# Score products of the second attention layer in 64-row tiles, on block-diagonal pairs of keys

## The chip, the cores and the metric

The kernel runs on one core of a Trainium2 chip. The metric is the device time of one execution in microseconds (us). The times of before are 384.46 us as the median of 3 runs (383.48 to 384.55).

## The reference, cut to what matters

Four layers run one after the other on `x` of 2048 tokens by 448 features: attention (layer 0), gated MLP (layer 1), attention (layer 2), gated MLP (layer 3). Both attention layers have the same weights, and so have both MLP layers. All inputs are bf16.

```python
x = x + A(layernorm(x));  x = x + B(layernorm(x))
x = x + A(layernorm(x));  x = x + B(layernorm(x))

def A(x):                       # H = 16 heads of 28, window W = 8, dilation 2
    q, k, v = split(x @ wqkv)
    idx = pos[:, None] - 2 * arange(8)          # 8 keys of each query
    logits = where(idx >= 0, q . k[idx] * 28 ** -0.5, -1e9)
    return (softmax(logits) . v[idx]) @ wo

def B(x):
    return ((x @ w_gate) * (x @ w_up)) @ w_down
```

A query looks at 8 keys at distances 0, 2, ... 14 behind it.

## The kernel before, in words

**Tokens.** Even tokens are stored first and odd tokens behind them, 1024 each (`HALF`), so that the dilated window becomes a window of 8 neighbours in each half. The 2048 stored tokens are cut into 17 query blocks (`qb_info`): block 0 of 128 queries, and 16 of 120 queries that look at 128 keys. Blocks 1 and 2, 3 and 4 and so on are handled in pairs: 9 groups in each attention layer, the first with one block. The block that crosses from the even to the odd half is called `STRADDLE`.

**Stages.** `SEQ` lists the jobs. `A00` is chunk 0 of layer 0, and so on. An attention chunk makes the transposed normalised input `xnT` (`ln_chunk`), the keys and queries (`qk_chunk`, matmuls of L362 on `WQK`), the values (`v_group`, L362 on `WV`), and then for each group the scores (`attn_front`, matmuls of L842), exp on ScalarE (L849), a product with a mask on VectorE (L859), the product with the values (`attn_back`, L879), the sum and the division (L890 to L917), and the output projection (`y_blocks`, L362 on `wo_g`). The MLP chunks (`b_chunk`) make gate and up products (L362 on `WGU`; 14 units to a chunk of 512 tokens), ScalarE copies the gate (L970), VectorE multiplies (L973), and the down product follows (L362 on `WD`, with L934 that adds to `x_sb`).

**Tiles of TensorE.** Feature dimension 448 is 7 times 64 rows. So nearly every product runs in 64-row tiles: two matmuls of 64 rows by 128 columns lie side by side, one in the upper and one in the lower half of the array, each writing a bank of its own (`twin`, `twin_blocks`). The transposes at the head (L638) have the same form, with 64 streamed columns. Scores are another form: 28 rows (one head) by 64 keys, in 32-row tiles, 64 matmuls to a pair of blocks, into four banks. The product with the values has 64 rows by 32 columns, 64 matmuls to a pair.

**Keys, queries, values.** `qk` holds both for all 2048 tokens, a head in 28 of each 32 partitions; the four rows between carry a part of the values, which goes to DRAM (`vt`, DMAs of L741) and comes back transposed. Head 4*hc + b stands in partitions 32*b, chunk hc. Values are copied out of PSUM by one instruction for a pair of blocks (L824).

**Order.** The code adds operations one after the other (`sc.add`); the number of an operation is its place in that list. The order on each engine is written out by hand in `ORD`, a list of numbers per engine, and `BANK` gives the PSUM banks. `44!v` is operation 44, and the letter tells which of its waits stands last. `253+349@24.30.42` is a burst (the 64 short matmuls of 253) in which operation 349, broken into strips of 32 columns (L365) or 32 rows (L369), is mixed at the places named. Every engine works its list strictly in order. `plan_waits` leaves out waits that others cover. The costs given with `sc.add` served to make the lists; at run time they do nothing.

**Head.** TensorE runs 18 matmuls on zeros (L535, operations 44 to 61): 15 before the first transposes of `xn` (110 and 114, blocks 0 and 1) and 3 behind them, then the first keys and queries (199 on). Those need the transposed input, copied out by ScalarE and VectorE (L646), and the weights in `WQK`, spread out of `stage` by 8 copies (L544, operations 62 to 69: row chunk c, half w; the first two units need the four of w = 0). Six of the copies are GpSimd's: its list has 63, 62, 64, 68, 69 and later 65 among 16 small operations that build the masks (L515, L519).

Of the kernel before, what the change touches and what calls it, by code (L numbers as in the profile page):

```python
# [7 lines left out]
S = 2048  # L8
# [47 lines left out]
FILL = 9  # L56
ORD = {
# [56 lines left out]

# [9 lines left out]
class Sched:  # L124
# [21 lines left out]
    def schedule(self):  # L146
# [29 lines left out]
        for e in self.ENGS:  # L176
            for x in ORD[e].split():
                ids, _, hint = x.partition("!")
                ids, _, cuts = ids.partition("@")
                ids, _, pre = ids.partition("~")  # L180
                burst, *hosts = [self.ops[int(i)] for i in ids.split("+")]
                pre = int(pre or 0)
                if pre:
                    for op in hosts:
                        take(op, e)
                    order[e].append((hosts, [(op, n) for op in hosts for n in range(2 * pre)], hint[:1]))
                    hint = hint[1:]
                    take(burst, e)
                else:
                    for op in (burst, *hosts):  # L190
                        take(op, e)
                seq = [(burst, n) for n in range(len(burst.ins))]
                if hosts:
                    strips = self.strips(x, hosts, pre, len(cuts.split(".")))
                    done = pre + len(strips) // len(hosts)
                    seq, a = [], 0
                    for i, z in enumerate([int(c) for c in cuts.split(".")] + [len(burst.ins)]):
                        seq += [(burst, n) for n in range(a, z)]
# [4 lines left out]
                order[e].append(([burst] if pre else [burst, *hosts], seq, hint))  # L203
# [194 lines left out]
def build(nc, A_x, A_wqkv, A_wo, B_w_gate, B_w_up, B_w_down, out):  # L398
# [35 lines left out]
    ones32 = sb([128, 128], bf, "ones32")  # L434
    MK = sb([128, 3, 72], bf, "MK")
    ident = sb([128, 128], bf, "ident")
# [263 lines left out]
    def qk_chunk(li, j, prio):  # L700
# [5 lines left out]
        if li >= 2:  # L706
            for qb in range(NQB):
                k0, nk, tok, nq = qb_info(qb)
                if k0 < c1 and tok + nq > c0:
                    war.append(("S", li - 2, qb))  # L710
# [43 lines left out]
    def v_group(li, qbs, prio):  # L754
# [19 lines left out]
        def out(which):  # L774
            return ps[:, bk[which], 0:nv]
# [340 lines left out]
```

## Time and profile before

| | |
|---|---|
| median of 3 runs | 384.46 us (383.48 to 384.55) |
| profiled execution | 384.47 us |
| its span in the trace | 382.7 us, so 1.8 us lie around the span |
| TensorE busy | 377.9 us |
| VectorE, ScalarE, GpSimd busy | 268.9, 198.7, 10.4 us |
| instructions | 14257 |

How to read it: the profile is of one execution. The span is from the first to the last instruction. A busy TensorE isn't TensorE at its peak, because matmuls overlap: the time that a stretch of matmuls costs is the distance from the start of its first one to the start of what follows. A timeline row has the start, the duration up to the end of the last of them, engine, line, operation, output and inputs, and the count; a row of groups has busy time and mean of one in ns; a row of windows has the window, its length and each engine's busy time with the count.

### The profile page before, as it was taken

The page shows a single profiled execution, that of the slowest core. Times are in us where ns is not written, and L with a number is a line of the kernel's source. Part 1 is how long each engine was busy: PE and PEld are TensorE (multiplying, and loading weights), DVE is VectorE, ACT ScalarE, POOL GpSimd, SP SyncE. Part 2 cuts the span into 40 slices and gives each one's busy share as a digit, 9 for nine tenths or more (in the row PEclk, how much of TensorE's full clock was granted, in tenths as well). Part 3 has the DMA queues.
Part 4 walks back from the last instruction along what each step waited for, and adds up shares of the span by engine and source line. Part 5 has one row for each costly group of instructions (what it writes and reads, how often), then busy time and mean ns, then how long its engine had stood idle before and what let it go on. Part 6 is the DMA issues. An engine that isn't in the chain of part 4 may idle for free.

```text
span 382.7 us, 14257 instructions
## 1 busy us (share of the span) xinstructions
PE 377.9 (99%) x6406; PEld 209.3 (55%) x6406; DVE 268.9 (70%) x595; ACT 198.7 (52%) x393; POOL 10.4 (3%) x42
## 2 busy tenths in 40 slices
PE   8999999999999999999999999999999999999997
PEld 3556477544555445445466677544555544445764
DVE  5986989788886584885868766666787786355413
ACT  4989986646635672345343664457435542124310
POOL 7210000000000000000000000000000000000000
PEclk9999999999999999999999999999999999999999
DMA  8967422500540026010411425120142005030003
GB/s 271 240 138 204 111 65 44 90 6 15 81 48 16 17 49 77 15 27 15 70 24 29 46 40 83 40 26 4 21 93 45 14 2 108 2 70 6 2 2 120
DMA packets 55103, 22.75 MB, mean 59 GB/s; under 512 B 46132, under 2 KB 54148, under 8 KB 55044
## 3 DMA queue, kind: packets, MB, share of 16 engines
q1 hardware_dynamic: 54612, 21.34, 27.8%
q8 instruction: 50, 0.82, 0.9%
q10 hardware_dynamic: 432, 0.52, 0.4%
q14 instruction: 9, 0.07, 0.1%
HBM read 8.54 MB, written 2.71 MB: 29 GB/s over the span
## 4 chain that ended last, share of the span: by engine, by line
PE 99%; ACT 0%; DVE 0%; issue 0%
PE ps L362 88%; PE ps L842 3%; PE ps L365 2%; PE ps L879 2%; PE ps L535 2%; PE ps L985 1%; PE ps L638 1%; ACT qk L732 0%; PE ps L369 0%; DVE x_sb L989 0%; DVE hT L499 0%; DVE eps_sb L499 0%
## 5 line engine op out<-in xcount | busy, mean ns | idle before, releaser
L362 PE MATMUL ps<-xnTb,WGU 64*128 64x512 bf16 (+1 forms) x1922 | 175.1, 333 | 0.0
L362 PEld LDWEIGHTS ps<-xnTb,WGU 64*128 64x128 bf16 x1922 | 92.6, 94 | 72.1 <-ACT g_sb L970 0.9
L970 ACT ACTIVATE g_sb<-ps 128x512 bf16<-128x512 f32 (+1 forms) x140 | 69.5, 510 | 99.6 <-PE ps L362 91.3
L973 DVE TENSOR_TENSOR hT<-g_sb,ps 128x512 bf16<-128x512 bf16 (+1 forms) x140 | 77.5, 575 | 43.5 <-ACT g_sb L970 42.3
L362 PE MATMUL ps<-WD,hT 64*128 64x448 bf16 x802 | 82.5, 349 | 0.0
L934 DVE TENSOR_TENSOR x_sb<-x_sb,ps 128x448 bf16<-128x448 bf16 x62 | 36.5, 615 | 40.0 <-PE ps L362 39.9
L362 PEld LDWEIGHTS ps<-WD,hT 64*128 64x128 bf16 x802 | 38.3, 94 | 33.9 <-DVE hT L973 0.2
L362 PE MATMUL ps<-xnTa,WQK 64*128 64x512 bf16 (+1 forms) x498 | 53.7, 352 | 0.2
L607 DVE BATCH_NORM_STATS2 st<-x_sb 128x6 f32<-128x448 bf16 x64 | 38.2, 612 | 1.8 <-DMA x_sb<-in_A_x_dram 1.6
L849 ACT ACTIVATE E_sb<-ps 128x1024 bf16<-128x1024 f32 (+1 forms) x36 | 34.1, 982 | 10.0 <-PE ps L842 9.5
L628 DVE TENSOR_SCALAR xn_sb<-x_sb,mv,rstd 128x512 bf16<-128x512 bf16 (+1 forms) x64 | 35.9, 569 | 3.5 <-ACT rstd L612 3.5
L362 PEld LDWEIGHTS ps<-xnTa,WQK 64*128 64x128 bf16 x498 | 22.9, 94 | 21.9 <-PE ps L362 1.2
L732 ACT ACTIVATE qk<-ps 128x1024 bf16<-128x1024 f32 (+1 forms) x28 | 25.7, 934 | 10.7 <-PE ps L362 10.1
L362 PE MATMUL ps<-wo_g,oT 64*128 64x448 bf16 x256 | 29.0, 349 | 0.1
L859 DVE TENSOR_TENSOR E_sb<-E_sb,MK 128x1024 bf16<-128x1024 bf16 (+2 forms) x40 | 23.6, 607 | 5.5 <-ACT E_sb L849 5.3
L905 ACT ACTIVATE R_sb<-R_sb 128x480 f32<-128x480 f32 (+1 forms) x34 | 20.2, 601 | 11.4 <-DVE R_sb L904 11.4
L917 DVE TENSOR_TENSOR oT<-O_sb,R_sb 128x480 bf16<-128x480 f32 (+3 forms) x36 | 21.9, 623 | 3.0 <-ACT R_sb L906 2.8
L904 DVE STREAM_SHUFFLE R_sb<-O_sb 128x480 f32<-128x480 f32 (+1 forms) x34 | 23.3, 693 | 0.0
L362 PE MATMUL ps<-WV,xnTa 64*128 64x336 bf16 (+3 forms) x252 | 23.2, 304 | 0.0
L610 ACT ACTIVATE lnv<-mv,eps_sb 128x2 f32<-128x2 f32 (+1 forms) x33 | 9.6, 295 | 22.6 <-DVE mv L609 22.5
L906 ACT ACTIVATE R_sb<-R_sb 128x480 f32<-128x480 f32 (+1 forms) x34 | 19.8, 599 | 0.1
L362 PEld LDWEIGHTS ps<-wo_g,oT 64*128 64x128 bf16 x256 | 12.2, 94 | 11.0 <-PE ps L362 0.5
(56 smaller groups left out, 193.7 us busy)
## 6 DMA issues: line engine op xcount, KB each, us to landing
out_dram<-x_sb SPq DMA_DIRECT2D x15, 112.0 KB, 1.8
WGU<-in_B_w_gate_dram SPq DMA_DIRECT2D x7, 224.0 KB, 4.2
WGU<-in_B_w_up_dram SPq DMA_DIRECT2D x7, 224.0 KB, 4.1
x_sb<-in_A_x_dram SPq DMA_DIRECT2D x3, 448.0 KB, 6.1
WD<-in_B_w_down_dram SPq DMA_DIRECT2D x2, 448.0 KB, 4.2
WD<-in_B_w_down_dram SPq DMA_DIRECT2D x2, 336.0 KB, 4.1
vt<-qk SPq DMA_DIRECT2D x42, 16.0 KB
xnTb<-xn_sb SPq DMA_TRANSPOSE x32, 3.0
```

Of the source, the lines that this page charges most:

```text
L362: return lambda E: E.matmul(out(), lhs(), rhs(), start=start, stop=stop)
L607: sc.add("dve", one(lambda E, B=B: E.bn_stats(st6[:, B, :], x_sb[:, B, :]), ("bn", li, B)), 525.0, deps=[("x", li - 1, B)] + ([("xn", li - ...
L628: sc.add("dve", one(lambda E, B=B, dst=dst, src=src: E.tensor_scalar(dst, src, mv[:, B, 0:1], rstd[:, B:B + 1], ALU.subtract, ALU.mult), ( ...
L732: return E.activation(dst, src, ACT.Copy) if hasattr(E, "activation") else E.tensor_copy(dst, src)
L849: return E.activation(E_sb[:, slot, 2 * hp:2 * hp + 2, 0:w], ps[:, b0:b0 + 2, 0:w], ACT.Exp, scale=SCALE)
L859: return E.tensor_tensor(e, e, m, ALU.mult)
L904: sc.add("dve", one(lambda E: E.stream_shuffle(R_sb[:, rs, 0:w], O_sb[:, os_, 0:w], [DH] * 32), ("Rs", li, qb)), dve_est(w) + 100.0, deps= ...
L905: sc.add("act", one(lambda E: E.activation(R_sb[:, rs, 0:w], R_sb[:, rs, 0:w], ACT.Ln), ("Rl", li, qb)), act_est(w, False), deps=[("Rs", l ...
L917: return E.tensor_tensor(oT[:, :, a % HALF:a % HALF + z - a], O[:, :, a - tok:z - tok], R_sb[:, rs, 0:w].rearrange("p (h n) -> p h n", h=4 ...
L934: sc.add("dve", one(lambda E: E.tensor_tensor(x_sb[:, B, :], x_sb[:, B, :], ps[:, bk[w], 0:D], ALU.add), ("x", li, B)), dve_est(D), deps=[ ...
L970: sc.add("act", one(lambda E, gs=gs, bk=bk: E.activation(g_sb[:, gs, 0:nt], ps[:, bk[0], 0:nt], ACT.Copy), ("G", li, j, fc)), act_est(nt), ...
L973: sc.add("dve", one(lambda E, gs=gs, bk=bk, fc=fc: E.tensor_tensor(hT[:, fc, hs, 0:nt], g_sb[:, gs, 0:nt], ps[:, bk[1], 0:nt], ALU.mult), ...
```

## The change

Layer 0 keeps its scores. In layer 2, and only there, `attn_front2` takes the place of `attn_front`:

- Two heads share a 64-row tile. The keys of both are written side by side into a 64 by 128 block, keys of the even head in one half of the columns and of the odd head in the other, with zeros elsewhere (a copy scaled by a 0/1 column `pm` for each partition). Each group needs four such copies, one for each half of its keys (c) and each head of a pair (t), 512 elements to a partition for a pair of blocks: 36 in all. By the new lists 22 are GpSimd's, 8 ScalarE's and 6 VectorE's. They go to a half of the key buffer that layer 2 no longer uses (its second 1024 tokens' keys are stored over the first ones), in two slots.
- The scores of a pair of blocks are 32 matmuls of 64 rows by 128 columns with 64 streamed columns, in two operations of 16 (one for each c) with two banks each, instead of 64 in one operation with four banks.
- For this the heads are put in another order (`head_at`), in the copies of the weights `WQK` (on ScalarE now two instructions) and in the loads of `wo`. In layer 2 the values are copied out of PSUM by three instructions instead of one, two of them with a shift by 64 partitions.
- The masks get new combinations (`MB`), written by 8 small DMAs on the SP queue; five small memsets make `pm`.
- Of the 18 matmuls on zeros, 12 stand before the first transposes and six behind. Five of the six are cut, so that they have 128, 64, 64, 512, 64 and 64 columns.
- Some lists of waits are longer (`readersA`, `xslot_users`).
- All lists of `ORD` and `BANK` are new. Operations 44 on have numbers higher by 13, in layer 2 by 5 more for each group before. GpSimd's list has, after operation 34, 13 small mask and memset operations, then seven weight copies (the four of w = 0 first), then the rest, then the 22 key copies. SP's list has the loads of `WV` ahead of the third load of `x`, and those of `WGU` among those of `wo`. 13 product-with-values bursts in all have another operation mixed in, where before 12 had, and one burst of scores.

```diff
+FILLN = {12: 128, 13: 64, 14: 64, 16: 64, 17: 64}
 ORD = {
...
+def head_at(hc, b):
+    return 8 * (b % 2) + 2 * hc + b // 2
...
+    memset("dve", pm[:], 0.0, "i_pm", 60)
+    for b in range(4):
+        sc.add("dve", one(lambda E, b=b: E.memset(pm[32 * b:32 * b + DH, b % 2:b % 2 + 1], 1.0), ("pm", b)), 60, deps=["i_pm"], prio=-38)
+    for n, (k, src, dst) in enumerate([(0, 0, 0), (1, 1, 1), (1, 0, 0), (1, 0, 1), (2, 0, 0), (2, 0, 1), (0, 1, 0), (0, 1, 1)]):
+        slot = (0, 0, 1, 1, 2, 2, 3, 3)[n]
+        plain_dma("sp", MB[64 * dst:64 * dst + 64, slot, :], MK[64 * src:64 * src + 64, k, :], ("mb", n), "d_mb", ...)
...
+        m = FILLN.get(n, 512)
+        ins = [(lambda E, m=m: E.matmul(ps[:, wb[0], 0:m], warm[:, 0:128], warm[:, 0:m], start=True, stop=True), ("warm", n))]
...
+        if li:
+            def odd(E):
+                dst = v_sb[0:nk, s0:s0 + n, 256:384].rearrange("p s (q e) -> p s q e", e=32)[:, :, :, 0:DH]
+                src = ps[0:nk, bk[1]:bk[1] + 1, 0:112] if split else ps[0:nk, bk[0]:bk[0] + 2, 224:VD]
+                return cp(E, dst, src.rearrange("p s (q e) -> p s q e", e=DH))
+            def even(E, lo):
+                dst = v_sb[lo:lo + 64, s0:s0 + n, 0:256].rearrange("p s (q e) -> p s q e", e=32)[:, :, :, 0:DH]
+                return cp(E, dst, ps[64 - lo:128 - lo, bk[0]:bk[0] + n, 0:224].rearrange("p s (q e) -> p s q e", e=DH))
...
+    def attn_front2(li, g, prio, slot, prev):
+        ks = g % 2
+        KB = qk[:, 0, :, HALF + 512 * ks:HALF + 512 * ks + 512].rearrange("p h (d c n) -> p h d c n", d=2, c=2)
+        for c in range(2):
+            bk = Banks(2, pair=True)
+            war = [("S2", li, g - 2, c)] if g >= 2 else old_readers(HALF + 512 * ks, HALF + 512 * ks + 512)
+            for t in range(2):
+                lo = 64 * (c if t else 1 - c)
...
+                        if hasattr(E, "activation"):
+                            return E.activation(dst, src, ACT.Copy, scale=pm[:, t:t + 1])
+                        return E.tensor_scalar(dst, src, pm[:, t:t + 1], None, ALU.mult)
+                sc.add(("pool", "dve", "act"), ins, {"pool": 200.0 * len(ins) + 256 * nd * 2.65, ...}, deps=[("QK", li, j, h) ...] + war + PMD, prio=prio)
+            for hc, d, p in [(hc, d, p) for hc in range(4) for d in range(nd) for p in range(2)]:
+                qs, o = qb_info(qbs[d])[2] + 56 * c, (hc * nd + d) * nc
+                ins.append((lambda E, ...: E.matmul(ps[:, bk[p], o:o + nc], KB[64 * p:64 * p + 64, hc, d, c, :], qk[64 * p:64 * p + 64, 1, hc, qs:qs + nc], start=True, stop=True), None))
+            sc.add("pe", ins, len(ins) * 14.7, deps=[("KB", li, g, c, t) for t in range(2)] + ..., mode=MAIN, acquire=bk, prio=prio)
+            def fe(E, c=c, bk=bk):
+                return E.activation(E_sb[:, slot, 2 * c:2 * c + 2, 0:w], ps[:, bk[0]:bk[0] + 2, 0:w], ACT.Exp, scale=SCALE)
...
+            lo = 64 * (c if li == 0 or b % 2 else 1 - c)
+            ins.append((lambda E, ...: E.matmul(ps[32 * b:32 * b + 32, bk[c], o:o + nc], vw, E_sb[lo:lo + 64, slot, 2 * c + b // 2 if li else b, o:o + nc],
+                                                               start=True, stop=True, tile_position=(lo, 32 * b)), None))
```

More of the change, by code (lines that the diff above doesn't have):

```diff
@@ L187, in schedule @@
                     hint = hint[1:]
[L188 to L192, printed above, removed]
+                for op in bursts if pre else bursts + hosts:
+                    take(op, e)
+                seq = [(op, n) for op in bursts for n in range(len(op.ins))]
                 if hosts:
@@ L698, in twin_blocks, with key_col, old_readers @@
         crossed(parts, deps, prio, pe_cols(D), acquire, keys[0][0] + "ps")
+    def key_col(li, t):
+        return t % HALF if li else t
+    def old_readers(a, z):
+        res = [("S", 0, qb) for qb in range(NQB) if qb_info(qb)[0] < z and sum(qb_info(qb)[2:]) > a]
+        return res + [("PW", 0, i) for i in chunks_of(0, a, z) if (0, i) not in NOPW]
     def qk_chunk(li, j, prio):
@@ L974, in b_chunk @@
                        deps=[("G", li, j, fc), ("Ups", li, j, fc)] + war, release=[(bk, 1)], prio=prio)
[L975 removed]
+        xslot_users[hs] = [(k, li, j, fc) for k in ("Gps", "Ups") for fc in range(FC)]
         users = []
```

121 lines of the change are left out of this document (88 added, 33 removed), and 10 rows, old and new, of the table ORD.

## The prediction

> **What bounds the kernel now.** I read the page first: the span, the busy times, the chain that ended last.
>
> ```profile
> span 382.7 us, 14257 instructions
> PE 377.9 (99%) x6406; PEld 209.3 (55%) x6406; DVE 268.9 (70%) x595; ACT 198.7 (52%) x393; POOL 10.4 (3%) x42
> ...
> PE 99%; ACT 0%; DVE 0%; issue 0%
> ```
>
> TensorE is the whole chain. It never waits long for anyone, so only two things can move the end: fewer or shorter TensorE steps, or a new wait. "Busy" doesn't say whether the steps are efficient. For that I read TensorE's timeline around one score burst of layer 2 and take distances from start to start.
>
> ```profile
> 177.08 0.59 PE L362 MATMUL ps<-WV,xnTa 64*128 64x336 bf16 x6
> 177.60 0.71 PE L842 MATMUL ps<-qk 28*64 28x64 bf16 x64
> 178.24 0.74 PE L362 MATMUL ps<-WV,xnTa 64*128 64x336 bf16 x8
> 178.82 0.35 PE L362 MATMUL ps<-wo_g,oT 64*128 64x448 bf16 x2
> ```
>
> Eight value matmuls take 178.82 - 178.24 = 0.58 us, so 0.145 for each two that lie side by side. The six ahead of the burst would be through after 0.435, at 177.515; the burst starts at 177.60. So 0.085 us are lost on the way in, and 178.24 - 177.60 = 0.64 on the burst. **One burst costs 0.725 us.** The reader is to see that a change of the tile form costs time which no idle column shows.
>
> Next, the same kind of reading for short 64-row matmuls, the transposes of the head:
>
> ```profile
> 20.23 0.81 PE L362 MATMUL ps<-xnTa,WQK 64*128 64x512 bf16 x6
> 20.88 0.28 PE L638 MATMUL ps<-ident,xn_sb 64*128 64x64 bf16 x8
> 21.00 1.03 PE L362 MATMUL ps<-xnTa,WQK 64*128 64x512 bf16 x8
> 21.86 0.40 PE L638 MATMUL ps<-ident,xn_sb 64*128 64x64 bf16 x16
> ```
>
> Eight long ones take 21.86 - 21.00 = 0.86, so the six before take 0.645, and 20.88 - 20.23 = 0.65: nothing is lost on the way in. Eight transposes take 0.12 us, 15 ns each. They have exactly the form of the new scores: 64 rows, 128 columns, 64 streamed.
>
> Last, the windows over the part in which layer 2 runs (120 to 300 us), for the room on the other engines:
>
> ```profile
> 120.00:160.00 40.00, 40.00 (x588) 19.70 (x586) 27.27 (x62) 19.49 (x38) 0.00 (x0) 1.00 0.25 35
> 160.00:215.00 55.00, 55.00 (x910) 31.64 (x906) 40.59 (x86) 26.78 (x55) 0.00 (x0) 1.00 0.17 31
> 215.00:300.00 85.00, 85.00 (x1568) 47.79 (x1569) 58.56 (x127) 44.93 (x83) 0.00 (x0) 1.00 0.28 45
> ```
>
> Columns are TensorE, its weight loads, VectorE, ScalarE, GpSimd. Of 180 us VectorE is busy 126.4 (53.6 free), ScalarE 91.2 (88.8 free), GpSimd not at all. TensorE is busy all of it.
>
> **The change, part by part.**
>
> *Scores of layer 2.* A pair's burst of 0.725 becomes 32 matmuls at 15 ns, 0.48 us, with no change of form: 0.245 less. Eight pairs give 1.96. The first group has half as many and longer columns; its gain lies between 0 and half of a pair's 0.245, and I take 0.1. **Minus 2.1 us.** I count the one burst that before mixes with other work like the rest.
>
> *Mixing of a burst in layer 0.* The product with values of operation 402 stood alone and is now mixed with another operation. Both kinds are in the trace:
>
> ```profile
> 76.44 1.69 PE L362 MATMUL ps<-xnTb,WGU 64*128 64x512 bf16 x14
> 78.06 0.68 PE L879 MATMUL ps<-E_sb,v_sb 64*32 64x64 bf16 x64
> 78.68 0.93 PE L362 MATMUL ps<-wo_g,oT 64*128 64x448 bf16 x8
> ...
> 114.33 1.03 PE L362 MATMUL ps<-xnTb,WGU 64*128 64x512 bf16 x8
> 115.29 0.28 PE L879 MATMUL ps<-E_sb,v_sb 64*32 64x64 bf16 x24
> ...
> 116.34 0.35 PE L362 MATMUL ps<-WD,hT 64*128 64x448 bf16 x2
> ```
>
> 14 gate/up matmuls are 7 times 0.215 = 1.505. Alone: 78.68 - 76.44 = 2.24, so the burst costs 0.735. Mixed into the same 14: 116.34 - 114.33 = 2.01, so 0.505. **Minus 0.2 us.** The other 12 stay mixed. In layer 2 heads of a burst alternate between the two row halves; eight tiles take turns as before, so I count no change.
>
> *Head.* TensorE, GpSimd, VectorE and ScalarE up to the first keys:
>
> ```profile
> 1.26 6.07 PE L535 MATMUL ps<-hT 128*128 128x512 bf16 x15 [1.26 <-DVE eps_sb L499]
> 7.26 0.41 PE L638 MATMUL ps<-ident,xn_sb 64*128 64x64 bf16 x16
> 7.60 0.82 PE L535 MATMUL ps<-hT 128*128 128x512 bf16 x3
> 8.40 2.94 PE L362 MATMUL ps<-xnTa,WQK 64*128 64x256 bf16 x42
> ```
> ```profile
> 2.62 0.24 POOL L515 TENSOR_SCALAR_AFFINE_SELECT hT<-hT 128x72 bf16<-128x72 bf16 x1
> 3.98 1.06 POOL L544 COPY WQK<-hT 128x448 bf16<-128x448 bf16 x2 [1.11 <-DMA hT<-in_A_wqkv_dram]
> 4.98 0.24 POOL L515 TENSOR_SCALAR_AFFINE_SELECT hT<-hT 128x72 bf16<-128x72 bf16 x1
> 5.82 0.56 POOL L544 COPY WQK<-hT 128x448 bf16<-128x448 bf16 x1 [0.59 <-DMA hT<-in_A_wqkv_dram]
> 6.72 0.56 POOL L544 COPY WQK<-hT 128x448 bf16<-128x448 bf16 x1 [0.34 <-DMA hT<-in_A_wqkv_dram]
> ```
> ```profile
> 5.27 0.38 DVE L628 TENSOR_SCALAR xn_sb<-x_sb,mv,rstd 128x512 bf16<-128x512 bf16 x1
> 5.95 0.57 DVE L628 TENSOR_SCALAR xn_sb<-x_sb,mv,rstd 128x512 bf16<-128x512 bf16 x1 [0.30 <-ACT rstd L612]
> ```
> ```profile
> 7.59 0.66 ACT L646 ACTIVATE xnTa<-ps 128x256 bf16<-128x256 bf16 x2 [1.21 <-PE ps L638]
> ```
>
> Block 1 is normalised at 5.95 + 0.57 = 6.52, but 15 matmuls on zeros hold its transposes until 7.26. With 12 of them (four fifths of 6.00 us from 1.26 on: 6.06) the transposes come at 6.5, up to 0.74 earlier. Then the weights are late next: 13 small operations stand ahead of the copies on GpSimd, at 0.24 or less about 3 us from 2.86, so to 5.9, and the four copies of w = 0 at 0.53 (1.06 for two) end near 8.0; transfers land at 3.98, 5.82 and 6.72, early enough. First keys near 8.0 instead of 8.40: 0.4 us. The next blocks come at VectorE's pace, whose work shrinks by nothing, and it gets `pm`'s memsets. Bounds: 0.3 lost, if the spreading copies with their finer pieces are slower, and 0.85 gained; I take **minus 0.4 us**. The three matmuls at 7.60 fill a wait for ScalarE (7.59 + 0.66 = 8.25); shortened they neither cost nor gain.
>
> *Key copies.* 36 are added, and each score half waits for two. The nearest rows:
>
> ```profile
> L544 POOL COPY WQK<-hT 128x448 bf16<-128x448 bf16 x6 | 3.2, 558 | 2.0 <-DMA hT<-in_A_wqkv_dram 2.0
> ```
> ```profile
> L970 ACT ACTIVATE g_sb<-ps 128x512 bf16<-128x512 f32 x41 | 24.0, 596 | 37.9 <-PE ps L362 35.3 <-DVE hT L973 2.5
> L824 ACT ACTIVATE v_sb<-ps 128x672 bf16<-128x672 f32 x4 | 2.9, 731 | 0.9 <-PE ps L362 0.9
> ```
>
> GpSimd: 558 ns for 448 elements is 0.64 for 512; the diff's own estimate is 200 + 2.65 x 512 = 1.56. 22 of them are 14 to 34 us on an engine with 180 free. ScalarE: 8 x 0.6 = 4.8. VectorE: 6 x 0.4 (the 5.27 row) = 2.4. All fit into the free time above. A score half that waits holds everything behind it on TensorE, which works its list in order: values, projections, gate/up units, whose ScalarE and VectorE steps wait in turn. Where it is closest, group 2, the new list has two gate/up units (1.5 us each) and value products between the last keys and operation 938, about 4 us, for four ScalarE copies of 0.6; before, the scores came right behind. No score of layer 2 has GpSimd's letter in the new list, so GpSimd's copies weren't expected as the last wait. Between 0 and the 4.2 us of the rival below I take **plus 0.3 us**.
>
> *Copies of values.* One copy of 0.73 becomes three, of 224, 448 and 448 elements: each below the 0.60 of 512, so 1.8 at most; nine times 1.1 is 10 us more at most on ScalarE and VectorE, inside 142 us free. Hidden, as PSUM banks are taken two at a time now where a score burst took four.
>
> *DMAs.* Eight mask loads and a new order on SP's queue:
>
> ```profile
> 177.09 2.35 SPq L741 DMA_DIRECT2D vt<-qk  x7
> ```
>
> At 0.34 each they hold SP 2.7 us in all, spread out, ahead of transposing loads that have slots for six blocks. Nothing, or 0.34 if one is caught. The masks are first needed near 128 us.
>
> *Sum:* -2.1 - 0.2 - 0.4 + 0.3 = -2.4. Span 382.7 - 2.4 = 380.3; with the 1.8 around it **382.1 us**. The profiled execution (384.47) is 0.01 from the median, so no correction.
>
> **A rule against the change.** Weight loads of 64 rows by 128 columns take 94 ns each on the profile's page:
>
> ```profile
> L362 PEld LDWEIGHTS ps<-xnTa,WQK 64*128 64x128 bf16 x498 | 22.9, 94 | 21.9 <-PE ps L362 1.2
> ```
>
> If two row halves loaded one after the other at that pace, a score matmul would cost 47 ns, not 15: 272 matmuls (8 x 32 + 16) x 32 ns = 8.7 us more, **390.8 us**. The transposes speak against it: eight such loads and matmuls in 0.12 us. The Trainium skill, "TensorE: Matmul & The Clock Gate", section "LDWEIGHTS (loading the stationary operand)", has weight loads last as long as the number of columns over 1.2 GHz; as an estimate from that, 107 ns for 128 columns and some 392 us for the kernel. The trace disagrees with that rule in the transposes' row (15 ns each), but no row so far shows a plain matmul of this form.
>
> **The rivals.**
>
> *Slower: GpSimd holds VectorE up.* The two rows of `xn` above are the same work: 0.38 alone, 0.57 while GpSimd's copy of 5.82 ran. 22 key copies come into a stretch where VectorE is 70% busy. If each costs TensorE the 0.19 us that the one in the head cost VectorE, 4.2 us come on top of a sum without the 0.3: 386.0. It decides from 0.12 us per copy (2.7 over 22: gain gone); at 0.18 the kernel is 0.3% slower. For it: in-order lists without slack on TensorE. Against: 53.6 us free on VectorE, and four gate buffers. The Trainium skill, "SBUF — State Buffer", section "SBUF: two separate sides", says the port pair that both engines share is locked for a whole instruction; by that, the wait of one VectorE step could be up to GpSimd's 0.64 to 1.56 us. The trace agrees that it waits, with 0.19.
>
> *It doesn't do what it says: the form still changes.* If each of the 17 score halves paid 0.085 going in and as much going out, 2.9 us come back: 385.0, within 0.3%.
>
> *Late keys.* If in 9 of the 17 score halves the keys come late by half a GpSimd copy (0.32 of 0.64), 2.9 us come in place of the 0.3: 384.7, within 0.3%.
>
> *The head gives more.* 0.85 instead of 0.4, and no stall: 381.3.
>
> **How the numbers follow.** About 0.3% (1.15 us) can be told from no change. Forecast 0.66 (381.0 to 383.3), more from the head and the order 0.06 (below 381.0): faster 0.72. Form still changes 0.06, late keys 0.08: same 0.14. GpSimd holds VectorE up 0.11, slow weights 0.03: slower 0.14. The range leaves out the slow cases and the tail below: 380.2 to 385.2.
>
> **What would show it.** Score rows of layer 2 in TensorE's timeline: 16 matmuls in 0.24 us, no gap ahead. First keys near 8.0. TensorE's idle column near 0 behind 24 us, with no wait on GpSimd. VectorE's mask products no longer than before while GpSimd copies. I am wrong if 16 scores take 0.4 or more, if TensorE waits for key copies or masks by more than 1 us in sum, or if the head starts no earlier than 8.4.

## The result and the profile after

| | before | after |
|---|---|---|
| median, 6 runs of each | 384.17 us (383.48 to 384.55) | 382.11 us (381.34 to 382.73) |
| ratio | | 0.9946 (95%: 0.9929 to 0.9962), so 1.5 to 2.7 us shorter |
| profiled execution | 384.47 us | 382.09 us |
| its span | 382.7 us | 380.0 us |

382.1 us was predicted. The two profiled executions are 2.4 us apart, the medians 2.1; the places below are of the profiled pair. The page of the changed kernel: span, busy times, chain by engine.

```profile
span 380.0 us, 13741 instructions
PE 374.3 (99%) x6116; PEld 209.8 (55%) x6116; DVE 274.2 (72%) x610; ACT 208.8 (55%) x412; POOL 46.0 (12%) x69
...
PE 92%; DVE 3%; DMA 3%; SPq 2%; issue 0%
```

TensorE has 290 matmuls fewer and is 3.6 us less busy; GpSimd took 35.6 us of new work. The chain is no longer TensorE alone: VectorE, DMA and SP's queue have a share. That is the first trace of new waits. What TensorE waits for is in its view of waits (total us, times, longest):

```profile
PE ps L982 <- DMA v_sb<-vt: 0.7, 1, 0.7
PE ps L982 <- DVE xnTa L665: 0.3, 1, 0.3
PE ps L657 <- DVE xn_sb L647: 0.3, 1, 0.3
```

Left out is the engine's first start (1.2 us; 1.3 before). Nothing in this view names a key copy or GpSimd. The 0.7 us is a load of values in layer 0, where the change has a new order and mask loads on SP's queue, but no new form. TensorE's timeline around one score burst of layer 2, and around the head:

```profile
177.63 2.11 PE L367 MATMUL ps<-xnTb,WGU 64*128 64x512 bf16 x18
179.58 0.40 PE L948 MATMUL ps<-qk 64*128 64x64 bf16 x16
179.81 1.68 PE L367 MATMUL ps<-xnTb,WGU 64*128 64x512 bf16 x14
```
```profile
6.76 0.29 PE L657 MATMUL ps<-cst,xn_sb 64*128 64x64 bf16 x8 [0.25 <-DVE xn_sb L647]
...
7.67 2.87 PE L367 MATMUL ps<-xnTa,WQK 64*128 64x256 bf16 x48
10.38 0.29 PE L657 MATMUL ps<-cst,xn_sb 64*128 64x64 bf16 x8
```

Sixteen scores last from 179.58 to 179.81, 0.23 us, 14.5 ns each. Ahead of them 18 gate/up matmuls, 9 times 0.215 = 1.935, would be through at 179.565: at most 0.015 us are lost on the way in, no more than the rounding of the rows. The two halves of a pair need 0.47 us plus next to nothing, where one burst of before cost 0.725. The first keys start at 7.67 instead of 8.40.

The windows over layer 2 (window, its length, busy us of TensorE, weight loads, VectorE, ScalarE, GpSimd, then the clock):

```profile
120.00:160.00 40.00, 40.00 (x546) 20.42 (x544) 32.51 (x67) 20.46 (x43) 3.18 (x2) 1.00 0.24 37
160.00:215.00 55.00, 55.00 (x848) 31.90 (x844) 39.99 (x92) 32.58 (x66) 7.77 (x5) 1.00 0.21 38
215.00:300.00 85.00, 85.00 (x1456) 48.56 (x1454) 61.40 (x131) 50.07 (x92) 23.72 (x17) 1.00 0.23 39
```

VectorE, ScalarE and GpSimd are busier by 7.5, 11.9 and 34.7 us in these 180, and TensorE still has no gap.

**Where the time came from.** In both kernels there are places at which the same bursts begin and at which, but for the filling with zeros and the scores of layer 2, the same matmuls have gone before (some of them in strips, mixed into bursts). Their starts can be subtracted. Three such places in the timeline of before:

```profile
23.26 0.70 PE L842 MATMUL ps<-qk 28*64 28x64 bf16 x64 [0.55 <-ACT qk L732]
...
99.18 0.71 PE L842 MATMUL ps<-qk 28*64 28x64 bf16 x64
...
136.26 0.34 PE L879 MATMUL ps<-E_sb,v_sb 64*32 64x72 bf16 x32
```

And in that of after:

```profile
21.77 0.70 PE L890 MATMUL ps<-qk 28*64 28x64 bf16 x64
...
98.48 0.73 PE L890 MATMUL ps<-qk 28*64 28x64 bf16 x64
...
135.51 0.34 PE L982 MATMUL ps<-E_sb,v_sb 64*32 64x72 bf16 x32
```

| stretch | changes by | after the place |
|---|---|---|
| head, to the second score burst | -1.49 us | -1.49 |
| to the score burst at 99.18 | +0.79 | -0.70 |
| to the first values of layer 2 | -0.05 | -0.75 |
| layers 2 and 3, to the end of the span | -1.95 | -2.70 |
| around the span (1.8 becomes 2.1) | +0.3 | -2.4 |

So the total was forecast well, and layer 2 gave about what was forecast of it (-2.0 from 99.18 us on; forecast -2.1 for the scores, +0.3 for stalls). But the head gave 1.1 us more than its 0.4, and two losses that weren't in the sum, between 23 and 99 us and around the span, took it back.

Most of the first loss falls at 77 us: SP's queue, then TensorE.

```profile
69.66 1.03 SPq L466 DMA_DIRECT2D cst<-MK  x1
70.73 1.23 SPq L781 DMA_TRANSPOSE v_sb<-vt  x1
72.42 1.11 SPq L466 DMA_DIRECT2D cst<-MK  x2
73.59 3.13 SPq L781 DMA_TRANSPOSE v_sb<-vt  x2
```
```profile
77.56 0.28 PE L982 MATMUL ps<-E_sb,v_sb 64*32 64x64 bf16 x24 [0.72 <-DMA v_sb<-vt]
```

Three of the eight mask loads (`cst<-MK`) stand between the loads of values, and hold the queue from 69.66 to 70.69 and from 72.42 to 73.53: 2.1 us for three, not 0.34 each. (The other five, earlier on, take 0.47 to 0.51 us each.) The product with values behind them waits 0.72 us. The other 0.07 us, and what the mixing gained in this stretch on top of them, I haven't taken apart.

### The profile page after: what moved, and what is told of

The parts are those of the page before. It is cut to its first block, busy times and chain, and to the rows that moved or that the text cites. A ratio compares the mean times of both kernels' runs of the same rounds, so it can differ in the third digit from the quotient of the medians.

```text
span 380.0 us, 13741 instructions
## 1 busy us (share of the span) xinstructions
PE 374.3 (99%) x6116; PEld 209.8 (55%) x6116; DVE 274.2 (72%) x610; ACT 208.8 (55%) x412; POOL 46.0 (12%) x69
## 3 DMA queue, kind: packets, MB, share of 16 engines
HBM read 8.54 MB, written 2.71 MB: 30 GB/s over the span
## 4 chain that ended last, share of the span: by engine, by line
PE 92%; DVE 3%; DMA 3%; SPq 2%; issue 0%
PE ps L367 84%; PE ps L370 2%; PE ps L982 2%; DMA x_sb<-in_A_x_dram 2%; DVE st L626 1%; PE ps L1088 1%; SPq L466 1%; PE ps L948 1%; DMA v_sb<-vt 1%; PE ps L890 1%; DVE xn_sb L647 1%; DVE xnTa L665 0%; DVE mv L628 0%; SPq L781 0%; DVE E_sb L907 0%
## 5 line engine op out<-in xcount | busy, mean ns | idle before, releaser
L367 PE MATMUL ps<-xnTb,WGU 64*128 64x512 bf16 (+1 forms) x1932 | 177.1, 333 | 0.0
L941 POOL TENSOR_SCALAR qk<-qk,pm 128x512 bf16<-128x512 bf16 (+1 forms) x24 | 34.7, 1460 | 217.9 <-ACT qk L761 176.4
L367 PE MATMUL ps<-xnTa,WQK 64*128 64x512 bf16 (+1 forms) x494 | 52.8, 352 | 0.2
L761 ACT ACTIVATE qk<-ps 128x1024 bf16<-128x1024 f32 (+1 forms) x31 | 28.0, 923 | 12.2 <-PE ps L367 12.1
```

Source lines behind the costliest of these rows:

```text
L367: return lambda E: E.matmul(out(), lhs(), rhs(), start=start, stop=stop)
L761: return E.activation(dst, src, ACT.Copy) if hasattr(E, "activation") else E.tensor_copy(dst, src)
L941: return E.tensor_scalar(dst, src, pm[:, t:t + 1], None, ALU.mult)
```

## The experiments

The theory after the result: the gain of layer 2 is the form of the scores, each change of tile form costing a fixed price; GpSimd's copies cost nothing; the mask loads on SP's queue cost 0.7 us at 77 us; the head's gain is the shorter filling ahead of the transposes. Rivals: the gain is the order of the lists and not the form; GpSimd's work is paid for by VectorE; the filling only fills waits. The runs came in three groups, each with runs of the kernel before on its chip: 384.48 us (11 runs) for the first four, 384.35 (17) for the next four, 384.57 (21) for the last three. Between groups the ratios compare better than the medians; the changed kernel's is 0.9946.

**1. Mask loads later.** In SP's list the three loads 56, 53 and 52 go behind the value loads 598, 533 and 604.

```diff
-... 450 56 598 53 52 533 604 662 ...
+... 450 598 533 604 56 53 52 662 ...
```

> The changed kernel with three of the eight mask loads (operations 56, 53, 52) moved on SP's list behind the value loads 598, 533 and 604 that they stand ahead of; the masks are needed some 50 us later. Theory (the trace of after: the burst of values at 77.56 waits 0.72 us for its transposed load, issued at 73.59 right behind two mask loads of 1.11 us together): the wait at 77 us goes, the value load is issued at about 72.4, 0.7 to 0.8 us less than the changed kernel, about 381.4 us. Rival (the load is late because its own source is late, or because SP is full anyway): the wait stays and the time is within 0.2 us of the changed kernel, 382.1.

Measured: 381.92 us (381.02 to 383.7), ratio 0.9936 (0.9915 to 0.9957). The queue and the burst in this run:

```profile
71.26 4.84 SPq L781 DMA_TRANSPOSE v_sb<-vt  x3
76.16 1.87 SPq L466 DMA_DIRECT2D cst<-MK  x3
```
```profile
77.12 0.28 PE L982 MATMUL ps<-E_sb,v_sb 64*32 64x64 bf16 x24
```

The wait is gone, and the three loads, now with nothing behind them that is due, take 1.87 us, 0.6 each. The two programs have the same TensorE list, so each weight load can be set beside its twin: at 72 us this run stands 0.36 us behind the changed kernel's profiled run, past the burst 0.35 ahead. That is 0.71 us from this one place. At the end of the span only 0.1 is left, since this run lost 0.3 us to a wait near 61 us and 0.25 near 282. So the trace shows the mechanism, but the median misses the theory's 381.4 us: the 0.2 us beside the changed kernel (0.4 by the ratios) lie within the scatter.

**2. The old form of the scores in the new order.** Each half of layer 2's scores as 32 matmuls of 28 rows by 64 columns; all else, copies of keys too, as changed.

```diff
-ins.append((lambda E, ...: E.matmul(ps[:, bk[p], o:o + nc], KB[64 * p:64 * p + 64, hc, d, c, :], qk[64 * p:64 * p + 64, 1, hc, qs:qs + nc], ...
+for t in range(2):
+    b, lo = 2 * p + t, 64 * (c if t else 1 - c)
+    ins.append((lambda E, ...: E.matmul(ps[lo:lo + 64, bk[p], o:o + nc], KB[32 * b:32 * b + DH, hc, d, c, lo:lo + 64], qk[32 * b:32 * b + DH, 1, hc, qs:qs + nc], ..., tile_position=(32 * b, lo)), None))
```

> The changed kernel, with order, key copies, masks and everything else as they are, but the scores of layer 2 again in 28 by 64 tiles: each half does 32 matmuls on the 28 rows and 64 columns of the blocks that aren't zero, instead of 16 on 64 by 128. Theory (a change of tile form costs 0.085 us going in, and a burst of 64 takes 0.64): the half bursts cost about 0.09 + 0.3 instead of 0.235, so 17 or 18 of them 2.4 to 3.0 us more than the changed kernel: 384.5 to 385.1. Rival (the gain of the change came from the head and the order of the lists, the form of the tiles is worth little): less than 1 us more, below 383.1.

Measured: 386.69 us (385.36 to 387.99), ratio 1.0057 (1.0037 to 1.0078): 4.3 us above the changed kernel by the two ratios, and slower than before. Its timeline at the same two halves:

```profile
179.78 1.24 PE L367 MATMUL ps<-xnTb,WGU 64*128 64x512 bf16 x10
180.95 0.44 PE L950 MATMUL ps<-qk 28*64 28x64 bf16 x32
181.33 1.68 PE L367 MATMUL ps<-xnTb,WGU 64*128 64x512 bf16 x14
...
192.81 0.71 PE L950 MATMUL ps<-qk 28*64 28x64 bf16 x64
193.44 0.74 PE L367 MATMUL ps<-WD,hT 64*128 64x448 bf16 x6
```

Ten gate/up matmuls end after 1.075, at 180.855; the burst starts 0.095 later and takes 0.38. A half costs 0.47 us instead of 0.23. Added up over all score bursts of layer 2, with what is lost ahead of them, that is 8.05 instead of 4.01 us (leaving out 0.4 us of waiting inside one burst): 4.0 of the 4.3. The rest isn't traced; in the profiled run, which is 0.3 us above the median, the wait for values at 78 us is also 0.4 us longer. The rival (the order makes the gain) falls. The size was expected smaller, and the reason is instructive: I had taken half of a 0.725 burst for each half, but part of a burst's cost is there whatever its length. The last two rows show it in this same run: at one place both halves of a pair stand next to each other, 64 matmuls in one go, and they take 0.63 us with 0.095 ahead, 0.73 in all, where two halves apart cost 0.94. So **about 0.21 us is the fixed price of one excursion to the other form**, and the matmuls themselves cost 8 ns each. Apart from this place the halves of the new list pay it twice as often. The new form pays next to nothing at each border, which is what lets the change cut the bursts in halves.

**3. GpSimd's key copies cut to one element.** The list stays, so do the waits; each of the 24 instructions writes one column.

```diff
+if CUR[0] == "pool":
+    src, dst = qk[:, 0, 0, cols[d or 0]:cols[d or 0] + 1], KB[:, 0, d or 0, c, lo:lo + 1]
```

> The changed kernel, but each of GpSimd's key copies handles one element of a partition instead of 256 or 512, so that the rest of these blocks keeps other keys: this part of the computation is left out, waits and order are the same. Theory (VectorE's mask products take 687 ns without and 688 with a key copy of GpSimd beside them, and TensorE waits for none): within 0.3 us of the changed kernel, 381.8 to 382.4. Rival (GpSimd's 35 us hold VectorE up through the port or delay the scores): 1 us or more less, below 381.1.

Measured: 382.48 us (381.8 to 383.35), ratio 0.9952 (0.9933 to 0.997): no shorter than the changed kernel. GpSimd's groups in the changed kernel, then here (busy us, mean ns of one):

```profile
L941 POOL TENSOR_SCALAR qk<-qk,pm 128x512 bf16<-128x512 bf16 x20 | 31.1, 1568 | 177.2 <-ACT qk L761 176.4 <-PE ps L948 0.8
```
```profile
L947 POOL TENSOR_SCALAR qk<-qk,pm 128x1 bf16<-128x1 bf16 x24 | 6.8, 304 | 242.6 <-ACT qk L765 189.8 <-DVE qk L765 43.3 <-PE ps L954 9.6
```

31.1 us of work, and 3.7 in four half copies (22 copies in 24 instructions), became 6.8, and nothing was gained; by the two intervals a gain over about 0.7 us is out. The traces narrow it down: weight load by weight load, this run and the changed kernel's stay 0.38 to 0.39 us apart from 100 to 278 us, and the key copies start between 125.9 and 273.2. The copies are hidden; 1.57 us each, they are at the upper of the two prices that the prediction named.

**4. The old filling in the changed kernel.** 15 matmuls on zeros ahead of the first transposes, all of full length.

```diff
-FILLN = {12: 128, 13: 64, 14: 64, 16: 64, 17: 64}
+FILLN = {}
-    "pe": "... 66 67 68 123!v 127!v 69 70 71 72 73 74 214!a ...
+    "pe": "... 66 67 68 69 70 71 123!v 127!v 72 73 74 214!a ...
```

> The changed kernel with the head's matmuls on zeros as before: 15 of 512 columns before the first transposes and three of 512 behind. Theory (the first transposes came at 7.26 then and at 6.22 now, first keys at 8.40 and 7.67): transposes again at about 7.25, first keys near 8.4, and 0.7 us of the 1.4 that the head gained by 23 us are given back: 382.8. If all of the head's gain hangs on it, 383.5. Rival (the head is paced by the arrival of x and by VectorE, the matmuls on zeros only fill waits): within 0.3 us of the changed kernel, 382.1.

Measured: 382.47 us (381.19 to 383.01), ratio 0.9943 (0.9923 to 0.9962): 0.4 us above the changed kernel by the medians, 0.1 below by the ratios, so the two expectations aren't told apart. In its profiled run the 15 matmuls were through at 6.24 us, 5.00 us after their start, where the same 15 took 6.00 in before; and the first keys waited 0.18 us for GpSimd's copies of the weights (7.89):

```profile
6.24 0.72 PE L657 MATMUL ps<-cst,xn_sb 64*128 64x64 bf16 x16
...
7.89 1.37 PE L367 MATMUL ps<-xnTa,WQK 64*128 64x256 bf16 x22 [0.18 <-POOL WQK L561]
```

How long the same filling takes differs by 1 us between these two runs, so one profile alone can't size it. By the windows TensorE has at most 4 of them in a us here until 5 us and 7 from 5 to 6, where in before it still has 4 from 5 to 6; the clock column reads 1.00 in both, so no run here shows why.

**5. The new filling alone, in the kernel before.**

```diff
-    "pe": "... 54 55 56 57 58 110!v 114!v 59 60 61 199!a ...
+    "pe": "... 54 55 110!v 114!v 56 57 58 59 60 61 199!a ...
+FILLN = {12: 128, 13: 64, 14: 64, 16: 64, 17: 64}
```

> The kernel before with the new head's filling alone: twelve instead of fifteen matmuls on zeros ahead of the first transposes, and those after them with 128 or 64 columns. Theory (the filling holds the head back): the first transposes stand at 7.26 us behind the fifteen and their normalised rows are there from 5.65, so they move to 6.2 to 6.9 us, the first key matmul from 8.40 to 7.8 to 8.1, and the time falls by 0.3 to 0.6 us: ratio 0.9984 to 0.9992. Rival (the filling only fills waits, the weight copies set the first keys): the first keys stay at 8.2 or later and the time stays within 0.2 us, ratio 0.9995 to 1.0005.

Measured: 383.97 us (383.66 to 384.35, 11 runs), ratio 0.9992 (0.9984 to 1.0001). 0.3 us, at the lower edge of what the theory gave; the interval takes in no change. The first keys came earlier than either expectation had them:

```profile
6.26 0.69 PE L640 MATMUL ps<-ident,xn_sb 64*128 64x64 bf16 x16
...
7.52 1.72 PE L363 MATMUL ps<-xnTa,WQK 64*128 64x256 bf16 x24
```

The transposes moved by 1.0 us and the first keys by 0.88 in the profiled pair, and set beside before, weight load by weight load, 0.66 of that is kept to the end. The wait of 0.55 us for ScalarE's copy of keys, which stood ahead of the second score burst before, is still here (0.5 us). In the changed kernel and all its variants 0.1 is left of it.

**6. Copies of the weights earlier on GpSimd.** In the changed kernel, ahead of the last mask selections.

```diff
-    "pool": "... 31 35 32 36 21 33 28 39 40 29 75 79 77 81 76 78 80 41 ...
+    "pool": "... 31 35 75 32 36 79 77 81 76 78 80 21 33 28 39 40 29 41 ...
```

> The changed kernel with GpSimd's copies of the query and key weights put ahead of the last mask selections, so that they start near 4.3 us instead of 5.34. Theory (the fourth of these copies, which ended at 7.62 us, releases the first keys at 7.67, and the copies that run beside the second normalisation make it 0.76 us instead of 0.38): the first keys come at 7.3 to 7.6 us with no wait on GpSimd, and the time falls by 0.1 to 0.4 us, 381.7 to 382.0 beside 382.1. Rival (the head's gate is the second normalised block, behind its x load and the clock): the first keys stay within 0.1 us of 7.67 or later, since both normalisations now run beside copies, and the time is the same within 0.2 us or up to 0.3 us longer.

Measured: 381.64 us (381.18 to 382.33, 5 runs), ratio 0.9934 (0.9923 to 0.9946). First keys at 7.32, as the theory has it; what is left of the wait on GpSimd is under 0.1 us. Set beside the changed kernel's profile this run is 0.31 us ahead until 67 us; then the wait for the values at 77 us grows from 0.72 to 0.94 and takes 0.22 of it. While a DMA ends last, what is gained ahead of it can be waited away there.

**7. Both moves**, of runs 1 and 6.

> The changed kernel with both moves: the three mask loads behind the value load of the first layer 0 burst of query block 11, and the weight copies ahead of the last mask selections. Theory (the mask loads' issues of 0.5 us each cost 0.7 to 0.9 us at 77 us, and the head some more): 381.0 to 381.6 us, ratio to the kernel before 0.991 to 0.9925, no wait of TensorE on the value load at 77 us. Rival (what is gained at 77 us is used up by waits that follow, as the end of the earlier run without the mask loads moved by 0.1 only): 381.7 to 382.2.

Measured: 381.64 us (380.77 to 383.48), ratio 0.994 (0.992 to 0.996). Its profiled run is 0.54 us ahead of the changed kernel's at 67 us, 1.01 ahead once past the burst at 77, and 0.9 ahead at the end of the span. The wait for the values there is 0.22 us: smaller than 0.72, not gone as the theory had it, since TensorE now comes earlier. Time and ratio lie just outside the theory's range. The median beats the changed kernel's by 0.5 us, but the intervals of the ratios overlap widely: I don't call it shown that this version is faster.

**8. One more semaphore, in the kernel before.** It asks for the 0.3 us around the span.

```diff
-["d_one", "d_stv"]
+["d_one", "d_stv", "d_mb"]
```

> The kernel before with one more semaphore that nothing uses, as the changed kernel has one for its mask loads. It asks where the 0.3 us outside the span come from (384.47 less 382.7 is 1.8 before, 382.09 less 380.0 is 2.1 after, the same in every run of each). Theory (the count of semaphores, cleared outside the span): time less span becomes 2.1. Rival (something else of the program, the mask loads or the longer lists): it stays at 1.8, and the time at 384.2 to 384.8.

Measured: one run, 385.77 us with a span of 384.0; around it 1.8. The theory falls. The run is 1.3 us longer than the kernel before in its profile and has 1.1 of it by 14 us, from the head: `x` landed later (4.00 us instead of 3.78 for the first statistics) and two copies of the weights, which waited for their DMA, came 1.5 us later (8.27 instead of 6.72). Nothing in the program explains that; one run of it can't say more than that the head scatters.

**9. 22 products on GpSimd alone, in the kernel before**, and **10. 150 of them.**

```diff
+@block.gpsimd
+def _(E):
+    ...
+    for n in range(22):                      # 150 in run 10
+        ...
+        E.tensor_scalar(scr[:, 1:9, :], scr[:, 0:1, :].to_broadcast([128, 8, 64]), sc1[:, 0:1], None, ALU.mult).then_inc(sems["d_mb"], 1)
```

> The kernel before, with 22 products of a tensor and a column (128 by 512 elements, bf16) put behind GpSimd's last operation, one after the other from about 15 us on, into memory that nothing reads; each waits for the one before. Theory (GpSimd's work costs the other engines nothing): 384.2 to 384.6 us, and VectorE's groups keep their means. Rival of the prediction (each holds VectorE up, 0.19 us per copy): 388.5 us. It also asks where the 0.3 us around the span come from: time less span 2.1 instead of 1.8 if a longer GpSimd program is the reason.

> The same with 150 of these products, so that GpSimd is busy from about 15 us to about 260 us. Theory (no cost): 384.2 to 384.8 us, VectorE's mean for the normalisation, the gated product and the mask product within 2% of before. Rival (0.19 us each): 413 us; if only VectorE's steps grow and its free time takes it in, the means rise by 10% or more and the time by less than 3 us.

Measured: 384.98 us (384.48 to 385.79), ratio 1.0011 (1.0002 to 1.0021), for 22; 385.11 us (384.6 to 385.89), ratio 1.0022 (1.0013 to 1.0032), for 150; 1.8 us around the span in both. VectorE's groups by shape in before, then with 150 products (mean ns of one behind the busy us):

```profile
L973 DVE TENSOR_TENSOR hT<-g_sb,ps 128x512 bf16<-128x512 bf16 x84 | 55.6, 681 | 25.9 <-ACT g_sb L970 24.8 <-PE ps L842 0.8
...
L628 DVE TENSOR_SCALAR xn_sb<-x_sb,mv,rstd 128x512 bf16<-128x512 bf16 x32 | 12.7, 408 | 1.3 <-ACT rstd L612 1.3
```
```profile
L975 DVE TENSOR_TENSOR hT<-g_sb,ps 128x512 bf16<-128x512 bf16 x84 | 55.4, 679 | 24.4 <-ACT g_sb L972 23.4 <-PE ps L844 0.8
...
L630 DVE TENSOR_SCALAR xn_sb<-x_sb,mv,rstd 128x512 bf16<-128x512 bf16 x32 | 15.7, 501 | 1.2 <-ACT rstd L614 1.2
```

And all mask products by themselves, with their shortest, median and longest duration in ns, in before and with 150 products:

```profile
L859 DVE TENSOR_TENSOR E_sb<-E_sb,MK x40: 412/683/694, 17.9 to 297.3; 128x1024 bf16<-128x1024 bf16 x28, 128x512 bf16<-128x512 bf16 x8, 128x576 bf16<-128x576 bf16 x4
```
```profile
L861 DVE TENSOR_TENSOR E_sb<-E_sb,MK x40: 418/678/1115, 17.2 to 297.4; 128x1024 bf16<-128x1024 bf16 x28, 128x512 bf16<-128x512 bf16 x8, 128x576 bf16<-128x576 bf16 x4
```

Neither theory holds as it stood; nearest is the third expectation of run 10, that some of VectorE's steps grow and its free time takes it in. Beside a GpSimd that hardly rests (busy 241 of the 255 us from 22.9 on) three of VectorE's forms get longer: the normalisation of 512 elements by 23% in the mean, single mask products by up to 0.42 us, while their median stays, and the product that makes `oT` out of two SBUF tensors (688 instead of 649 ns in the mean). The gated product, which reads PSUM, doesn't change, and nor does the normalisation of 896 elements (729 and 731 ns). VectorE's sum rises from 268.9 to 274.9 us, 0.04 us for each of the 150; TensorE pays 0.85 us by the ratio, 0.006 for each. The rival's 0.19 us for each copy is out by a factor of 30. By the ratios half of the cost comes with the first 22, which lie beside layer 0, where both profiles have a new wait of TensorE, 0.3 us for a mask product at 41 us.

**11. Eight small DMAs alone, in the kernel before.** 64 rows of 144 bytes each, from DRAM into memory that nothing reads.

```diff
+EXTRA = {366: [0], 507: [1], 577: [2], 431: [3, 4], 519: [5], 520: [6, 7]}
...
+if e == "sp" and op.idx in EXTRA:
+    for x in EXTRA[op.idx]:
+        E.dma_start(...).then_inc(sems["d_mb"], 16)
```

> The kernel before with eight DMAs of 64 rows by 144 bytes on SP's queue, into memory that nothing reads, three of them right ahead of the value loads 519 and 520 of query block 11, the other five earlier. Theory (a small DMA holds the queue 0.5 us, and a transposing load behind it is late): SP's rows show 0.5 us for each, TensorE waits 0.5 to 1.0 us for the values at 78 us, and the time is 384.8 to 385.4. Rival (0.34 us each, taken in by the slack of the loads): no wait, 384.2 to 384.6. Time less span 2.1 instead of 1.8 if these DMAs are the reason for the 0.3 us around the span.

Measured: 392.3 us (392.0 to 393.77), ratio 1.0213 (1.0191 to 1.0235); 1.8 us around the span. Much more than either theory, and the wait isn't where it was expected: TensorE waits not for values but for the normalised input of the next gate/up units (`xnTb`), whose transposing loads stand on SP's queue behind the value loads 519 and 520. Two of the eight DMAs stand right ahead of the second of these loads (431). The profiled run is the longest of the four, 1.5 us above their median.

The last two loads of `xnTb`, on SP in before and here, then TensorE and a window here:

```profile
68.15 2.67 SPq L631 DMA_TRANSPOSE xnTb<-xn_sb  x2
```
```profile
72.50 1.22 SPq L351 DMA_DIRECT2D scr<-in_A_wo_dram  x2
...
76.06 3.56 SPq L640 DMA_TRANSPOSE xnTb<-xn_sb  x2
```
```profile
81.33 3.17 PE L369 MATMUL ps<-xnTb,WGU 64*128 64x512 bf16 x14 [6.65 <-DMA xnTb<-xn_sb]
84.29 1.52 PE L369 MATMUL ps<-wo_g,oT 64*128 64x448 bf16 x8
85.64 1.67 PE L369 MATMUL ps<-xnTb,WGU 64*128 64x512 bf16 x14
```
```profile
81.00:85.00 4.00, 3.67 (x18) 1.31 (x20) 0.00 (x0) 0.47 (x1) 0.00 (x0) 0.50 0.13 28
```

A DMA of this kind holds the queue for 0.5 to 0.6 us (two in 1.22), as in run 1; the first one took 1.23. The queue is through with the two loads of `xnTb` at 79.62 instead of 70.82, TensorE stands still for 6.65 us, and the column of the clock (the third from the right) has fallen to 0.50 by then and stays there until past 85 us: the 14 gate/up matmuls take 84.29 - 81.33 = 2.96 us instead of 1.5, and the eight behind them 1.35 instead of 0.76. Weight load by weight load the loss is 0.5 us before that place and 9.2 behind it: 6.65 of waiting, 2.05 of half clock. The eight issues add up to 5.3 us and the loads came 8.8 later; the rest I haven't taken apart.

## Why the prediction was right, and where it was wrong

**Scores of layer 2: right.** Forecast 15 ns each and no change of form; measured 14.5 ns and at most 0.015 us on the way in. All score bursts of layer 2, with what is lost ahead of them, add up to 6.15 us in the trace of before (0.73 for each pair, 0.37 for the first group, 0.66 for the one that is mixed) and to 4.01 in that of after (sixteen halves of 0.23, 0.29 for the first group): -2.1, as forecast. Run 2 shows that it is the form. With that the rival of the slow weights (47 ns each) is out: 16 loads of 64 rows by 128 columns and their matmuls pass in 0.23 us. By the rule that the prediction named from the Trainium skill, "TensorE: Matmul & The Clock Gate", section "LDWEIGHTS (loading the stationary operand)", they would take, as an estimate, 1.7 us one after the other, or half of that in the two row halves at once; the measurement decides against it for this form.

**Key copies: right in kind, too dear.** Forecast +0.3 from stalls; TensorE's waits name no key copy, and run 3 gives nothing back. From the first values of layer 2 on the time moved by -1.95, 0.1 less than the scores of the eight pairs alone (-2.05), which isn't traced to a place.

**GpSimd holds VectorE up: out.** The mask products of layer 2 in the changed kernel, beside 24 key copies, in the same view as in run 10:

```profile
L963 DVE TENSOR_TENSOR E_sb<-E_sb,cst x19: 412/686/855, 132.0 to 292.5; 128x1024 bf16<-128x1024 bf16 x15, 128x576 bf16<-128x576 bf16 x2, 128x512 bf16<-128x512 bf16 x2
```

The median is what it was; the longest is 0.17 us above the rest. There is an effect, and runs 9 and 10 bound it. The Trainium skill, "SBUF — State Buffer", section "SBUF: two separate sides", limits it to VectorE's fast modes and steps with two SBUF inputs. The three forms that got longer and the gated product that didn't agree with that; why the normalisation of 896 elements stayed as it was is open. But the page has the port pair locked for a whole instruction. Under 1.6 us instructions that follow each other almost without a break (run 10), the median mask product would have to show it, and it doesn't; nor do mask products start later (31 to 34 ns behind the exp that they had waited for, with and without GpSimd's work). In the head it does lie on the path, beside GpSimd's copies of the weights; VectorE and GpSimd in the changed kernel:

```profile
5.26 0.38 DVE L647 TENSOR_SCALAR xn_sb<-x_sb,mv,rstd 128x512 bf16<-128x512 bf16 x1
...
5.94 0.76 DVE L647 TENSOR_SCALAR xn_sb<-x_sb,mv,rstd 128x512 bf16<-128x512 bf16 x1 [0.29 <-ACT rstd L631]
```
```profile
5.34 3.79 POOL L561 COPY WQK<-hT 128x448 bf16<-128x448 bf16 x7
```

The second normalisation takes twice the first, and the transposes of block 1 wait 0.25 us for it.

**Head: the step that was mis-sized.** "First keys near 8.0 instead of 8.40" became 7.67, and the second burst came 1.49 us earlier, not 0.4. The first keys: the 13 small operations on GpSimd were through at 5.34 instead of 5.9, so that the four copies behind them released the first keys 0.33 us earlier than forecast. That makes 0.73 of the 1.49. The other 0.76 lies between the first keys and the second burst, a stretch for which the prediction had no term. TensorE in before, then in the changed kernel:

```profile
11.29 0.29 PE L638 MATMUL ps<-ident,xn_sb 64*128 64x64 bf16 x8
...
22.39 0.32 PE L879 MATMUL ps<-E_sb,v_sb 64*32 64x72 bf16 x32
```
```profile
21.34 0.32 PE L982 MATMUL ps<-E_sb,v_sb 64*32 64x72 bf16 x32 [0.28 <-DVE xnTa L665]
```

The first 42 key matmuls took 11.29 - 8.40 = 2.89 us in before, 0.138 for each two; the first 48 of the new order take 10.38 - 7.67 = 2.71, 0.113 for each two. That is about 0.5 us; what held them up in before isn't taken apart. And from the product with values to the second score burst it is 0.87 us in before and 0.43 here: the wait of 0.55 us for ScalarE's copy of keys stood in the profile of before, in a row that I did not read, because I had followed the head only up to the first keys, and the new order has 0.10 there. About 0.2 us were lost elsewhere, above all in a new wait of 0.28 us ahead of the values. The filling, which I took for the cause, is worth 0.3 to 0.4 us in the medians of runs 4 and 5, with intervals that take in none, and the head of one program scatters by more than that from run to run (runs 4 and 8).

**Mixing of a burst: too high.** The burst at 77 us is the one. In run 1, where it doesn't wait, 14 gate/up matmuls, the burst and eight of the output projection take 78.40 - 75.52 = 2.88 us; alone, in the trace of before, from the 76.44 of the prediction's row to 79.44, where the eight are through, 3.00. That is -0.12, not -0.2.

**DMAs: the step that failed.** "Nothing, or 0.34 if one is caught", at 0.34 each. A mask load holds SP's queue for 0.5 to 0.6 us, once for 1.03, three stand ahead of value loads with no slack for that, and TensorE waits 0.72 us; with the three moved (run 1) it doesn't. The price came from the `vt` stores, which are another transfer; the slack was taken from slots for six blocks, but here it was the queue that decided when a load started, not a free slot. Run 11 shows how little slack there is elsewhere on that queue.

**Around the span: +0.3, open.** It is 2.05 to 2.18 us in every run of the changed kernel and its variants and 1.76 to 1.87 in every one of before's variants (1.8 in before's profile). Another semaphore, a longer GpSimd program and eight more DMAs don't make it (runs 8 to 11). The prediction took 1.8 for granted.

The total was right because the scores were, and because an underestimated gain in the head met two losses of nearly its size. The second half of that was luck.

## What to carry to other kernels

Price a change of tile form per excursion as well as per matmul: here about 0.21 us each, so fewer and longer excursions help as much as shorter matmuls, and a form that needs none can be cut as finely as the rest of the order likes. A small DMA on a queue that works in order can cost the loads behind it its issue time (0.5 to 0.6 us here); before adding one, look in the queue's rows for what it would push back and when that is due. And when an order is replaced, read the waits of the old profile over the whole stretch that is reordered: a wait that the new list happens to drop is a gain like any other, and no step of the change names it.

## What the runs showed of the hardware

After a standstill of 6.65 us (run 11) TensorE ran at half its clock for some 4 us, which cost 2.05 us on top of the wait; the Trainium skill, "TensorE: Matmul & The Clock Gate", section "What's actually happening", gives about 3.4 us for losing the clock and as much for getting it back; here it was gone within the 6.65 us and back some 4 us after the restart. GpSimd's product of a tensor and a column takes 1.57 to 1.69 us in the means (changed kernel, runs 9 and 10) for 512 bf16 elements in a partition, nearly three times its plain copy of 448 (0.56). Sixteen score matmuls in 64-row tiles start 14.5 ns apart; going to 32-row tiles and back has a fixed price of about 0.21 us (run 2). A single step of VectorE between SBUF tensors can be 0.42 us longer beside it, most are not, and the gated product that reads PSUM was not (681 and 679 ns; run 10).
